# Another order for converting w_out, and six transfers on another queue, in a DeltaNet and FFN kernel

## The chip, the cores and the metric

The kernel runs on one core of a Trainium2 chip, as one launch. The metric is device time in microseconds. Three executions of the kernel before took 726.48, 727.93 and 732.02 us; their median is 727.93.

## The reference

The first half is a DeltaNet attention: for each of 4 x 8 heads a 48 x 48 state is carried over 768 time steps. The second half is a feed-forward net on the result, with a quick GELU between its two matrices.

```python
k_n = k / (norm(k) + 1e-6)
for t in range(768):
    y[t]  = q[t] @ state
    v_old = state.T @ k_n[t]
    state = state + beta[t] * outer(k_n[t], v[t] - v_old)
x = y as (3072 tokens, 384)
h = x @ w_in                    # 384 x 2048
out = (h * sigmoid(1.702 * h)) @ w_out   # 2048 x 384
```

The weights `w_in` and `w_out` arrive in 64-bit floating point. The engines compute in 32 bits, so the kernel converts each weight itself, from the two 32-bit words of its 64.

## The kernel before, in words

**The attention.** Time is cut into 6 chunks of 128 steps. A chunk and a batch make a *unit*, 24 in all, with 8 heads each (from the second chunk on, a unit takes half a chunk of two batches). Within a unit the recurrence is a triangular system per head: Gram products of the keys (`gram`, tile `G`) give the matrix, whose 32 x 32 diagonal blocks are sent through memory (`Nd`) into the tile `NT`, one block per partition, and inverted there on VectorE (`invert`: tiles `NT`, `P`, `YB`, some 60 steps). The inverses come back through memory (`Yd`) as `XB`. Then the blocks are solved one after the other: TensorE multiplies by `XB` into `psU`, ScalarE copies the result into `VU`, TensorE subtracts its part from the later blocks (`psV`, in the first chunk), ScalarE copies that into `VU`, and so on. One such round is called a hop here. The first four units are solved in two pairs, units 0 and 1 in one loop of eight hops (`path`), 2 and 3 in the next (`later`); each loop closes with `put_out`, which multiplies with the queries (`psY`) and adds into the state `ST`. Before a unit's keys are used they are divided by their norms: VectorE sums squares (`ssq`), GpSimd takes the root (`rn`), VectorE inverts it, and ScalarE or VectorE scales the keys `KN`.

**The FFN.** `hidden` multiplies 256 tokens (`xT`) by `w_in` into tiles `ph`, two rows of 128 features at a time, and ScalarE applies the GELU into `gT`. `both_written` and `written` multiply `gT` with `w_out` into `po`. In the later slots (`seven`) half of these products are done by a seven-product scheme that needs differences of blocks of `w_out`; GpSimd forms them (`combined`, line 986, into `TW`). FFN work fills TensorE wherever the attention makes it wait.

**The weights.** `w_out` is 16 blocks of 128 rows. A block of raw words takes twice the space of the converted block. Raw words therefore lie in one of two sorts of places: inside `w_out` itself, in the part of it that is converted later (`inside`: blocks 3, 4, 5, 6, 7, 12, 13), or in tiles that other data has left (`outside`: 0, 8, 11 in a tile of the tag `xT`; 1, 9, 14 and 2, 10, 15 in two tiles of the tag `M`, which unit 0 to 2 use too). `order` lists the blocks as they are converted; 4 with 5 and 6 with 7 are one piece of twice the size. A conversion is six steps: a mask (VectorE), a Relu that shifts the exponent (ScalarE), and four more on VectorE. `conversions` interleaves two pieces: the first mask of the next piece comes ahead of the last two steps of the present one, and its Relu with it. When a piece is done, `fetches` issues the transfer of the block that takes its place.

**What sets the order.** Each engine works through its own queue in program order. Most instructions are recorded in the order of the Python code (`tc.keep_in_program_order`, the helper on line 123). The conversions and the second inversion form one background generator (`background`): all pieces up to the eighth block, then `invert(1)`, then the other pieces. `fill(us)` draws so many estimated microseconds from it, so the numbers in the `fill` calls decide behind which hop a conversion step stands, on VectorE and on ScalarE alike. Operations that are not pinned (line 986, 107, 115) may be placed earlier. Transfers are issued by SyncE (`sync`), by GpSimd (`other_queue`) or by ScalarE (`beside`); a transfer that must wait for its place to be free holds up those behind it in the same queue. The functions that the change touches:

Of the kernel before, what the change touches and what calls it, by code (L numbers as in the profile page):

```python
# [18 lines left out]
def kernel(  # L19
# [21 lines left out]
    B, H, S, D = q.shape  # L41
# [9 lines left out]
    NB = C // BS  # L51
# [5 lines left out]
    HF, HM = FC // 2, DM // 2  # L57
# [24 lines left out]
    QP = [cpool.tile([128, H, DP], F32, name=f"QP{i}") for i in range(2)]  # L82
# [7 lines left out]
    def place(dst, n):  # L90

        return dst[n if n < B else n % 2] if dst is QP else dst[n % len(dst)]
# [3 lines left out]
    def segments(n):  # L96

        c, m = units[n]
        if n < B:
            return [(slice(0, C), m, slice(c * C, (c + 1) * C))]  # L100
        at = c * C + m // 2 * CH
        return [(slice(u * CH, (u + 1) * CH), m % 2 * 2 + u, slice(at, at + CH)) for u in range(2)]

    def load(n, pairs, dma=nc.sync.dma_start):
        for dst, src in pairs:
            for rows, b, t in segments(n):
                dma(  # L107
                    out=place(dst, n)[rows, :, 0:D],
                    in_=src[b, :, t, :].rearrange("h p d -> p h d"),
                )  # L110
# [10 lines left out]
    def pinned(op):  # L121

        return lambda *a, **kw: tc.keep_in_program_order(op(*a, **kw))  # L123
# [12 lines left out]
    sync, beside = pinned(nc.sync.dma_start), pinned(nc.scalar.dma_start)  # L136
# [17 lines left out]
    def warm(n, after=None):  # L154
        ps = ps_moe.tile([128, 256], F32, tag="moe", name="ps_warm")
        if after is not None:
            after(ps[:, 0:1], 0.0)
        for _ in range(n):
            pe.matmul(ps, lhsT=ones[:, 0:128], rhs=ones, start=True, stop=True)
# [11 lines left out]
    def as_raw(words, shape):  # L171
        a, b = shape
        return words.rearrange("p (j n o) -> p j n o", j=a, n=b)

    def as_rows(raw):
        return raw.bitcast(moe_w_in.dtype).rearrange("p j n o -> p j (n o)")
# [35 lines left out]
    places, slots = {}, {}  # L212
    inside = {3: 6, 4: 8, 5: 10, 6: 12, 7: 14, 12: 14, 13: 10}
    outside = {0: "xT", 8: "xT", 11: "xT", 1: "M", 9: "M", 14: "M", 2: "M2", 10: "M2", 15: "M2"}
    order = [0, 1, 2, 3, 4, 5, 6, 7, 8, 13, 9, 10, 12, 11, 14, 15]

    def fetch_out(f):

        if f in outside:
            slot = outside[f]  # L220
            if slot not in slots:
                slots[slot] = wk.tile([128, 2 * DM], I32, tag=slot[:2].strip("2"), name="raw", bufs=4 if slot[0] == "M" else 3)
            words = slots[slot]
        else:
            words = raws[:, inside[f] * DM : (inside[f] + 2) * DM]
        places[f] = as_raw(words, (1, DM))
        sync(out=as_rows(places[f])[:, 0], in_=moe_w_out[f * 128 : (f + 1) * 128, :])

    def conversion(dst, raw, shape):

# [47 lines left out]
    done = set()  # L278

    def conversions():  # L280

        whole = list(pieces())

        def begin(i):
            dst, raw, shape, name = whole[i]
            ops = conversion(dst, places[name[1]] if raw is None else raw, shape)
            return ops, next(ops)

        after, cost = begin(0)
        next(after)  # L290
        yield cost
        for i in range(len(whole)):
            ops = after
            yield next(ops)
            yield next(ops)
            if i + 1 < len(whole):
                after, cost = begin(i + 1)
                yield cost
                next(after)
            yield next(ops)  # L300
            cost = next(ops)
            done.add(whole[i][3])
            fetches.pop(whole[i][3], lambda: None)()
            yield cost

    fetches = {
        ("in", 1): lambda: fetch_in(3, js=(2,)),
        ("in", 3): lambda: [fetch_out(f) for f in (4, 5, 6, 7)],
        ("in", 4 * KC - 1): lambda: fetch_out(3),
        ("out", 4): lambda: fetch_out(13),  # L310
        ("out", 6): lambda: fetch_out(12),
    }
# [3 lines left out]
    def background():  # L316

        converting = conversions()
        while ("out", order[HF - 2]) not in done:
            yield next(converting)  # L320
        yield from invert(1)
        done.add("inverse")
        yield from converting

    behind = background()

    def fill(us):
        while us > 0:
            us -= next(behind, us)
# [126 lines left out]
    def gram(n):  # L456

        return gram_whole(n) if n < B else gram_halves(n)
# [44 lines left out]
    def turn(n):  # L503
        kTs[n] = wk.tile([128, NP, 128], F32, tag="kT", name="kT", bufs=5)
        transposed(home(n), kTs[n])

    def load_diagonal(n, Nd, dma):

        b = units[n][1]
        dma(  # L510
            out=NT[b * NB * H : (b + 1) * NB * H].rearrange("d i k -> d (i k)"),
            in_=Nd.rearrange("(d r) -> d r", r=BS * BS),
        )
# [15 lines left out]
    def send_blocks(n, others=(), dma=sync):  # L529

        G = ready[n][2]
        Nd = dram.tile([H * C * BS], F32, tag="Nd", name="Nd", bufs=4)
        to = Nd.rearrange("(h p k) -> p h k", p=C, k=BS)
        for blk in range(NB):
            u = slice(blk * BS, (blk + 1) * BS)
            k = u if n < B else slice(blk % 2 * BS, (blk % 2 + 1) * BS)
            (beside if blk in others else dma)(out=to[u], in_=G[u, :, k])  # L537
        return Nd
# [543 lines left out]
    def written(c, b0, gT):  # L1082

        for i in range(HB):
            b = b0 + i
            po = ps_moe.tile([128, DM], F32, tag="moe", name="po")
            for f in range(FC):
                pe.matmul(
                    po, lhsT=gT[f // FQ][:, f % FQ, i * C : (i + 1) * C], rhs=w_out[:, f, :],
                    start=(f == 0), stop=(f == FC - 1),  # L1090
                )
                if f % 2 == 1 and f < FC - 1:
                    yield 1.3
            o = wk.tile([128, DM], F32, tag="o", name="o")
            act.copy(o, po)
            nc.sync.dma_start(out=out[b * S + c * C : b * S + (c + 1) * C, :], in_=o)
            yield 1.3
# [54 lines left out]
    def together(solves, belows):  # L1152

        solves = [(X, blk) for X, blk in solves if X]
        belows = [(X, blk) for X, blk in belows if X]
        psU = bank("psU") if solves else None
        psRs = [bank("psR") if X.n >= B else None for X, blk in belows]
        for h in range(H):
            for X, blk in solves:
                X.solve(blk, h, psU)  # L1160
            for (X, blk), psR in zip(belows, psRs):
                X.below(blk, h, psR)
        for X, blk in solves:
            X.solved(blk, psU)
        for (X, blk), psR in zip(belows, psRs):
            X.rest(blk, psR)
# [79 lines left out]
    other_queue = pinned(nc.gpsimd.dma_start)  # L1246
    betas = beta.rearrange("b h (c k j) -> (b h) c k j", k=NB, j=BS)
    for blk in range(NB):
# [3 lines left out]
        out=YB, in_=YB, compare_op=ALU.not_equal, fill=1.0, base=0,  # L1252
# [38 lines left out]
    for at in range(B):  # L1291
        for u in range(2):
            for half_ in range(2):
                lane = at * BS + u * 2 + half_
                other_queue(
                    out=bL[lane : (at + 1) * BS : NB],
                    in_=betas[(at % 2 * 2 + u) * H : (at % 2 * 2 + u + 1) * H, 1:, at // 2 * 2 + half_, :],
# [30 lines left out]
    def put_out(s):  # L1328
        s.queries()
        s.outputs(True, lambda: fill(1.7))  # L1330
        steps.pop(s.n)
# [4 lines left out]
    for i in range(2 * NB):  # L1336
        together(*next(path))
        if i in (1, 3):
            turn(B + HB + i // 2)
        if i in (4, 5):  # L1340
            gram(B + HB + i - 4)
            Ndx.append(send_blocks(B + HB + i - 4))
        if i < 2 * NB - 1:
            warm(NU if i == 2 else NU // 2 if i in (1, 3, 4, 5) else 2 * NU // 3)
        fill(2.1)
    put_out(pair[0])
    for X in pair[2:]:
        X.gather()
    load_diagonals(Ndx)
# [2 lines left out]
    fill(1.9)  # L1352
    put_out(pair[1])
    load(8, ((KN, k),), sync)
    for f in range(1, 3):
        fetch_out(f)
    for n in range(B, B + 2):
        load(n, ((QP, q),), sync)

    ffn = []  # L1360

    def feed(n=1):
        for _ in range(n):
            while ffn and next(ffn[0], None) is None:
                ffn.pop(0)
# [3 lines left out]
    for i in range(1, 2 * NB):  # L1369
        together(*next(later))  # L1370
        if i < 4:
            warm(NU if i < 3 else NU // 2)
        if i > 2:
            feed()
        fill(2.7)
    for s in pair[2:]:
        put_out(s)
        feed()
# [42 lines left out]
        fill(0.1)  # L1421
    for n in (2 * B, 2 * B + 1):
        load_diagonal(n, Nds[n], sync)
    fill(4)
    queue = [both, written(*units[HB], gTs[1])]
    early_banks.close()
    late["one"] = ctx.enter_context(
# [40 lines left out]
```

## Time and profile before

| | before |
|---|---|
| median of 3 executions | 727.93 us |
| the profiled execution | 727.72 us |
| its span | 726.0 us |
| mean granted TensorE clock | 0.971 |
| TensorE, matmuls | 679.5 us busy, 94% of the span |
| VectorE | 457.3 us, 63% |
| GpSimd | 255.9 us, 35% |
| ScalarE | 236.8 us, 33% |

How to read the rows of the profile: a row of a timeline is start, length (both in us), engine, line, operation, tiles as out<-in, partitions and elements, and how many instructions were merged (x). A bracket at its end gives the idle time of the engine just ahead of it and what ended that. A row of the chain of waits is start, length, and what the chain passes through. A row of the stage table is the stretch, its length, then for TensorE matmuls, TensorE weight loads, VectorE, ScalarE and GpSimd the busy us with their instructions in brackets, then the granted TensorE clock as a share of full speed, the busy share of the DMA engines, and GB/s. A matmul in 32 bits appears as two records, so a row of six is three matmuls. PE is TensorE, DVE VectorE, ACT ScalarE, POOL GpSimd, SP SyncE; SPq rows are the issuing of transfers.

### The profile page before, as it was taken

Reading aid. Unit: us, or ns where it says so; the run is one execution under the profiler, and the core shown is the slowest. Engines: PE = TensorE matmul, PEld = TensorE weight load, DVE = VectorE, ACT = ScalarE, POOL = GpSimd, SP = SyncE. Lnnn points to the kernel's source line nnn. Section 1 sums busy time; section 2 is a strip of 40 time slices with the busy share of each in tenths; the row PEclk is TensorE's granted clock in tenths of the full one; section 3 lists DMA queues with packets and bytes.
Section 4 is the critical chain, followed back from the end, with each engine's and each line's share of the span. In section 5 each row is a group of like instructions: output and inputs, shape, how many; then the busy total and the mean of one; then the engine's idle time right before and its main releaser. Section 6 shows DMA issues by size and latency. Waiting matters only on the chain.

```text
span 726.0 us, 20454 instructions
## 1 busy us (share of the span) xinstructions
PE 679.5 (94%) x8787; PEld 583.7 (80%) x8787; DVE 457.3 (63%) x869; ACT 236.8 (33%) x565; POOL 255.9 (35%) x267
## 2 busy tenths in 40 slices
PE   9188969989899999999999999999999999999997
PEld 7156758765567898898988888988988988989997
DVE  4799839984476499398498497696694892110000
ACT  3363635371233413413313323333233223222120
POOL 6085002030146652642652642732621402304032
PEclk9677989999999999999999999999999999999999
DMA  9897553342122312314213224123123111000100
GB/s 170 144 184 157 161 147 81 76 97 71 34 63 48 73 34 62 65 30 85 42 36 82 39 36 93 27 44 74 38 44 60 34 26 31 7 23 2 28 0 23
DMA packets 129179, 46.66 MB, mean 64 GB/s; under 512 B 118848, under 2 KB 123584, under 8 KB 129088
## 3 DMA queue, kind: packets, MB, share of 16 engines
q1 hardware_dynamic: 125280, 39.89, 26.9%
q0 software_dynamic: 2624, 5.07, 3.2%
q8 instruction: 69, 1.13, 0.7%
q10 hardware_dynamic: 1184, 0.39, 0.2%
q14 instruction: 22, 0.18, 0.1%
HBM read 33.13 MB, written 11.01 MB: 61 GB/s over the span
## 4 chain that ended last, share of the span: by engine, by line
PE 50%; DVE 30%; DMA 7%; issue 4%; ACT 4%; SPq 2%; POOL 2%; DVEq 0%; ACTq 0%; POOLq 0%
PE ph L123 21%; PE po L123 16%; DVE P L123 12%; DVE YB L123 6%; PE four L123 4%; DVE NT L123 3%; DMA NT<-Nd 3%; PE psU L123 3%; PE ps_warm L123 3%; DVE VU L123 2%; DVE w_out L123 2%; PE psT L123 2%; DMA Nd<-G 2%; PE psR L123 1%; SPq L537 1%
## 5 line engine op out<-in xcount | busy, mean ns | idle before, releaser
L123 PE MATMUL ph<-xT,w_in 128*128 128x256 f32 x1152 | 259.8, 383 | 1.8 <-ACT gT L123 1.5
L123 PEld LDWEIGHTS ph<-xT,w_in 128*128 128x128 f32 x1152 | 216.3, 191 | 33.0 <-ACT gT L123 1.9
L123 PE MATMUL po<-w_out,gT 128*128 128x192 f32 (+1 forms) x720 | 139.2, 348 | 8.7 <-DVE o L123 5.0
L986 POOL TENSOR_TENSOR gT<-gT 128x512 f32<-128x512 f32 x80 | 105.7, 1330 | 102.2 <-ACT gT L123 68.1
L123 PEld LDWEIGHTS po<-w_out,gT 128*128 128x128 f32 x720 | 118.5, 191 | 21.9 <-issue 7.4
L123 DVE TENSOR_TENSOR P<-NT,YB 64x2 f32<-64x2 f32 (+9 forms) x200 | 123.7, 619 | 5.8
L123 ACT ACTIVATE gT<-ph 128x512 f32<-128x512 f32 x90 | 53.6, 597 | 144.3 <-PE ph L123 143.0
L123 DVE TENSOR_REDUCE YB<-P 64x2 f32<-64x2 f32 (+9 forms) x200 | 81.8, 409 | 6.9
L123 PE MATMUL po<-TW,gT 128*128 128x192 f32 x480 | 82.3, 328 | 0.5 <-ACT o L123 0.5
L123 PEld LDWEIGHTS po<-TW,gT 128*128 128x128 f32 x480 | 78.0, 190 | 1.8 <-ACT o L123 1.1
L123 ACT COPY VU<-psU 32x384 f32<-32x384 f32 x96 | 45.1, 470 | 54.1 <-PE psU L123 48.2
L852 POOL TENSOR_SCALAR_AFFINE_SELECT M<-M 64x512 f32<-64x512 f32 x40 | 29.7, 742 | 89.6 <-ACT M L123 88.3
L123 DVE TENSOR_TENSOR o<-o,po 128x192 f32<-128x192 f32 x40 | 13.8, 346 | 73.8 <-PE po L123 44.5
L123 DVE TENSOR_TENSOR VU<-VU,psR 32x384 f32<-32x384 f32 x40 | 22.1, 554 | 41.3 <-PE psR L123 40.6
L123 PEld LDWEIGHTS psU<-VU,XB 32*32 32x32 f32 x1536 | 28.5, 106 | 20.5 <-ACT VU L123 10.1
L123 DVE TENSOR_TENSOR NT<-NT,bL 64x1024 f32<-64x1024 f32 (+1 forms) x9 | 12.0, 1328 | 47.3 <-DMA NT<-Nd 47.3
L107 POOL DMA_DIRECT2D KN<-in_k_dram x24 | 17.0, 711 | 69.6 <-PE four L123 69.6
L123 PE MATMUL psU<-VU,XB 32*32 32x48 f32 x1536 | 33.7, 204 | 7.9 <-ACT VU L123 7.9
L123 DVE TENSOR_TENSOR VU<-VU,four 128x384 f32<-128x384 f32 x19 | 10.5, 552 | 45.2 <-issue 33.2
L346 POOL TENSOR_TENSOR rn<-ssq,half 128x8 f32<-128x8 f32 x12 | 22.1, 1846 | 47.1 <-DVE ssq L123 47.1
L123 ACT COPY xT<-four 128x256 f32<-128x256 f32 (+1 forms) x40 | 13.1, 328 | 75.9 <-DVE ST L123 73.5
L123 ACT COPY M<-four 128x512 f32<-128x512 f32 x19 | 11.1, 586 | 78.5 <-DVE VU L123 69.7
(133 smaller groups left out, 788.6 us busy)
## 6 DMA issues: line engine op xcount, KB each, us to landing
QP<-in_q_dram SPq DMA_DIRECT2D x40, 96.0 KB, 2.8
VU<-in_v_dram SPq DMA_DIRECT2D x40, 96.0 KB, 3.7
out_dram<-o SPq DMA_DIRECT2D x40, 96.0 KB, 2.2
raw<-in_moe_w_out_dram SPq DMA_DIRECT2D x9, 384.0 KB, 3.7
NT<-Nd SPq DMA_DIRECT2D x24, 128.0 KB, 2.4
XB<-Yd SPq DMA_DIRECT2D x24, 128.0 KB, 2.6
Yd<-NT SPq DMA_DIRECT2D x22, 128.0 KB, 2.1
Nd<-G SPq DMA_DIRECT2D x86, 32.0 KB, 1.7
```

The source lines that it names most:

```text
L107: dma(out=place(dst, n)[rows, :, 0:D], in_=src[b, :, t, :].rearrange("h p d -> p h d"),)
L123: return lambda *a, **kw: tc.keep_in_program_order(op(*a, **kw))
L346: nc.gpsimd.tensor_tensor(rn, ssq, half, op=ALU.pow)
L537: (beside if blk in others else dma)(out=to[u], in_=G[u, :, k])
L852: nc.gpsimd.affine_select(out=M, in_=M, compare_op=ALU.is_gt, fill=0.0, base=0, pattern=[[0, H], [1, CH]], channel_multiplier=-1,)
L986: (engine or nc.gpsimd).tensor_tensor(o, a, b, op=op)
```

## The change

The order of conversion becomes 0, 4 and 5, 3, 1, 6 and 7, 2, and then as before: the pieces 4 and 5, and 3, whose raw words lie inside `w_out`, move ahead of 1 and 2. The background loop waits for the eighth entry of the order and not the seventh, since a single block now stands last among the first eight. Blocks 1 and 2 and the queries of units 4 and 5, which SyncE fetched behind the first pair of units, are now fetched by GpSimd's queue, earlier in the code: the queries and block 1 behind the seventh hop of the first pair, block 2 behind unit 0's `put_out`. Two fill amounts change: 2.7 to 2.3 in the second pair's loop (seven times), and 4 to 8 ahead of the slots.

```diff
-    order = [0, 1, 2, 3, 4, 5, 6, 7, 8, 13, 9, 10, 12, 11, 14, 15]
-
-    def fetch_out(f):
+    order = [0, 4, 5, 3, 1, 6, 7, 2, 8, 13, 9, 10, 12, 11, 14, 15]
+
+    def fetch_out(f, dma=sync):
...
-        sync(out=as_rows(places[f])[:, 0], in_=moe_w_out[f * 128 : (f + 1) * 128, :])
+        dma(out=as_rows(places[f])[:, 0], in_=moe_w_out[f * 128 : (f + 1) * 128, :])
...
-        while ("out", order[HF - 2]) not in done:
+        while ("out", order[HF - 1]) not in done:
...
+        if i == 2 * NB - 2:
+            for n in range(B, B + 2):
+                load(n, ((QP, q),), other_queue)
+            fetch_out(1, other_queue)
         fill(2.1)
     put_out(pair[0])
+    fetch_out(2, other_queue)
     for X in pair[2:]:
         X.gather()
...
     load(8, ((KN, k),), sync)
-    for f in range(1, 3):
-        fetch_out(f)
-    for n in range(B, B + 2):
-        load(n, ((QP, q),), sync)
...
         if i > 2:
             feed()
-        fill(2.7)
+        fill(2.3)
...
-    fill(4)
+    fill(8)
     queue = [both, written(*units[HB], gTs[1])]
```

## The prediction

> **What bounds the kernel now.** I start with the stage table (busy time per engine, granted clock, DMA share), because a share over the whole span mixes stages with different limits.
>
> ```profile
> 94.00:103.00 9.00, 2.75 (x52) 2.12 (x45) 2.32 (x6) 1.56 (x3) 0.00 (x0) 0.86 0.85 178
> 103.00:113.00 10.00, 10.00 (x146) 7.76 (x140) 5.73 (x13) 5.58 (x11) 0.99 (x1) 0.79 0.42 142
> 160.00:190.00 30.00, 25.59 (x166) 14.54 (x165) 16.89 (x37) 8.03 (x18) 1.54 (x2) 0.99 0.21 53
> 190.00:400.00 210.00, 207.09 (x3040) 176.91 (x3042) 149.91 (x276) 66.69 (x161) 94.90 (x91) 0.99 0.28 57
> 400.00:640.00 240.00, 237.40 (x3403) 214.47 (x3396) 158.03 (x291) 71.71 (x172) 88.79 (x81) 1.00 0.21 42
> 640.00:726.00 86.00, 81.93 (x576) 75.56 (x575) 4.48 (x12) 15.32 (x35) 20.10 (x16) 0.99 0.06 14
> ```
>
> The first number behind each length is TensorE's. From 190 us on it is busy 526.4 of 536 us, so what starts earlier at 190 ends earlier at 726, microsecond for microsecond. Before that there is a hole: at 94 to 103 us TensorE works 2.75 of 9 us, VectorE 2.32, ScalarE 1.56, GpSimd nothing, while the DMA engines are 0.85 busy. Everybody waits for a transfer. The timelines of VectorE, ScalarE, TensorE and SyncE and the chain of waits (the row with "DMA raw") say which one.
>
> ```profile
> 92.93 0.36 DVE L123 TENSOR_SCALAR raw<-raw 128x384 int32<-128x384 int32 x1
> 100.61 0.36 DVE L123 TENSOR_SCALAR w_out<-raw 128x384 int32<-128x384 int32 x1 [7.31 <-DMA raw<-in_moe_w_out_dram]
> 101.00 0.62 ACT L123 ACTIVATE w_out<-w_out,low 128x384 int32<-128x384 int32 x1 [7.96 <-DVE w_out L123]
> 101.64 0.47 ACT L123 COPY VU<-psU 32x384 f32<-32x384 f32 x1
> 94.95 1.46 PE L123 MATMUL ph<-xT,w_in 128*128 128x256 f32 x6
> 102.66 0.28 PE L123 MATMUL psU<-VU,XB 32*32 32x48 f32 x1 [6.25 <-ACT VU L123]
> ```
>
> ```profile
> 89.53 4.63 SPq L123 DMA_DIRECT2D xT<-last  x6
> 94.26 1.35 SPq L123 DMA_DIRECT2D KN<-in_k_dram  x2
> 95.66 1.09 SPq L123 DMA_DIRECT2D raw<-in_moe_w_out_dram  x2
> 96.80 3.33 SPq L123 DMA_DIRECT2D QP<-in_q_dram  x4
> 100.22 1.28 SPq L123 DMA_DIRECT2D w_out<-in_moe_w_out_dram  x1
> ```
>
> ```profile
> 95.66 4.93 DMA raw<-in_moe_w_out_dram
> ```
>
> Block 1 of w_out, second to be converted, is only issued at 95.66, behind eight other transfers in SyncE's queue, and lands 4.93 us later. VectorE waits for it, ScalarE's Relu of the same block waits for VectorE, and behind that Relu in ScalarE's queue stands the copy of U without which the next solve hop of units 2 and 3 can't start: TensorE idles 6.25 us. That hole is the first place to look for a gain.
>
> **The change part by part.** TensorE's order is the same in both programs; what moves is the order on VectorE and ScalarE, and six transfers.
>
> *Blocks 4 and 5 second.* VectorE takes them up at 93.3, where block 0's third step, the row at 92.93, ends. Their words were fetched long before:
>
> ```profile
> 73.14 1.79 SPq L123 DMA_DIRECT2D w_out<-in_moe_w_out_dram  x4
> DMA to landing us min/median/max: 3.1/6.1/8.4
> 107.95 1.49 PE ph L123 x6
> 110.24 1.51 PE ph L123 x6
> 111.66 0.86 PE L123 MATMUL psU<-VU,XB 32*32 32x48 f32 x16
> 104.09 2.93 PE L123 MATMUL ph<-xT,w_in 128*128 128x256 f32 x6
> ```
>
> Issued by 74.93, landed by 83.3 even at the slowest 8.4, wanted at 93.3. Their Relu now stands behind the two copies that the next hop needs, so that hop starts when TensorE has done its half tile of the FFN: 94.95 + 1.46 = 96.41 in place of 102.66, **6.25 us** earlier. Then the clock: hop plus half tile take 110.24 - 107.95 = 2.29 us once it is back, but the three from 102.66 to 111.66 took 9.00 us, as the half tile at 104.09 took 2.93 and not 1.49. Without the hole they take 6.87, so the last hop starts at 103.3, **8.4 us** earlier. (The Trainium skill, "TensorE: Matmul & The Clock Gate", Part 1, says that about 3.4 us without activity halve the clock. The 0.86 and 0.79 above agree, and by it any new wait shorter than that costs only its own length.)
>
> *Block 3 third.* The raws and queries leave SyncE's queue, so block 3's fetch moves from 100.22 into block 1's old place, 95.66, and with that row's 4.93 us lands at 100.6. One VectorE step and its Relu (0.36 and 0.62, the rows at 100.61 and 101.00) end at 101.6. That Relu stands ahead of the copy behind the hop of 96.41 + 2 x 2.29 = 101.0, which ends at 101.8. So it costs nothing, with 0.2 us of cover: at the slowest landing, 8.4, the copy is 3.3 us late; at 3.1 nothing is gained, since TensorE sets the pace. I take 0.
>
> *VectorE up to the inversion.* The same eight blocks stand ahead of it, with the same busy time.
>
> ```profile
> 108.19 0.56 DVE L123 SCALAR_TENSOR_TENSOR w_out<-raw,w_out 128x384 int32<-128x384 int32 x1 [3.96 <-ACT w_out L123]
> 113.22 1.60 DVE L123 SCALAR_TENSOR_TENSOR w_out<-w_out 128x768 int32<-128x768 int32 x1 [0.29 <-ACT w_out L123]
> 122.56 1.22 DVE L123 TENSOR_TENSOR NT<-NT,bL 128x1024 f32<-128x1024 f32 x1
> 127.05 0.54 DVE L123 TENSOR_REDUCE ssq<-ksq 128x8 f32<-128x384 f32 x1
> 151.72 1.22 DVE L123 TENSOR_TENSOR NT<-YB,bL 128x1024 f32<-128x1024 f32 x1
> ```
>
> 7.31 + 3.96 + 0.29 = 11.6 us of waiting go. In their place I find, step by step along the new order: 1.3 for the Relu of 4 and 5 (behind the two copies, done at 96.3), 2.4 for block 3 (98.2 to 100.6), 1.2 for the two sums into the state, which wait for ScalarE's copies behind each unit's last solve, 0.4 for block 2's Relu behind a Gelu: 5.3. One sum of key squares (0.5) now stands ahead too. The inversion starts 11.6 - 5.3 - 0.5 = 5.8 us earlier, at 116.8. It lasts 152.94 - 122.56 = 30.4, plus one more small step on a norm, some 0.35: it ends at 147.6 and not 152.9.
>
> *Norms ahead of conversions.* Seven fills of 2.3 for 2.7 let VectorE's background work run 2.8 us less far ahead, so the steps of the key norms come earlier among it. Before, the last norm, at 157.87, stood 4.9 us behind the inversion, after block 8's and half of block 13's conversion; now it follows it directly, at 147.9.
>
> ```profile
> 157.87 0.17 DVE L123 TENSOR_SCALAR rn<-rn 128x8 f32<-128x8 f32 x1
> 133.07 1.56 PE L123 MATMUL ph<-xT,w_in 128*128 128x256 f32 x6 [1.47 <-ACT gT L123]
> 157.90 0.69 PE L123 MATMUL psG<-kT 48*64 48x64 f32 x32 [1.29 <-ACT kT L123]
> 159.92 0.81 PE L123 MATMUL po<-w_out,gT 128*128 128x384 f32 x2
> 161.85 9.94 PE L123 MATMUL po<-w_out,gT 128*128 128x384 f32 x30 [1.12 <-ACT TW L123]
> 171.72 0.87 PE L123 MATMUL psU<-VU,XB 32*32 32x48 f32 x32
> ```
>
> From that norm to the big run of output products is 161.85 - 157.87 = 4.0 us (scale the keys, evict Gram blocks, a Relu, the last Gelu). So the products could start at 147.9 + 4.0 = 151.9. TensorE must be there too: it was ready at 160.73; less 8.4, less the 1.47 at 133.07 (ScalarE's scaling waited for a norm that now comes after three inversion steps and not ten), it is ready at 150.9. The later one holds; with 0.2 for the wait for kT, which stays about as it was, the products start at **152.1, 9.7 us earlier**. The new slots' first solves follow 9.9 us behind, at 162; the inversion's result, needed there, lands some 7 us behind its end as before, at 155.
>
> ```profile
> PE po L123 <- DVE w_out L123: 2.6, 2, 1.9
> ```
>
> *Fill 8 for 4 ahead of the slots* makes up for the fills dropped earlier: in both programs three Relus (of 13, 9, 10) stand between the inversion and the first copy of the slots. What they hold up is that copy; they are done at 156, the copy is due at 163: 6 us of cover. So the ping-pong of products and conversions behind it, where TensorE waits 2.6 of the 4.4 us that it idles from 160 to 190, comes back unchanged: 0; were it gone, 2.6 would be gained.
>
> *GpSimd's queue.* It gets four query loads and two raws.
>
> ```profile
> 104.31 0.99 POOL L986 TENSOR_TENSOR TW<-w_out 128x384 f32<-128x384 f32 x1 [38.96 <-DVE w_out L123]
> 54.05 4.08 DMA TW<-in_moe_w_in_dram
> 66.00:68.00 2.00, 1.72 (x56) 1.32 (x43) 1.97 (x4) 0.49 (x1) 0.00 (x0) 1.00 0.50 74
> 68.00:70.00 2.00, 0.65 (x48) 0.65 (x52) 1.97 (x3) 1.87 (x4) 0.00 (x0) 0.93 0.18 24
> ```
>
> GpSimd idles 38.96 us up to 104.31, so queries and block 1 go out as it falls idle, at 65.4, into DMA engines that are 0.50 and 0.18 busy, and land by about 75 (its own queue's 4.08 us, doubled). Block 2's place is unit 0's M, read until 85: it lands by 93 and is wanted at 111.5. Queued behind it on GpSimd are only differences of w_out, due after 103. I take 0; the bounds are up to 1 us lost if the extra transfers delay the hops of 69 to 80, and 0.5 gained if SyncE's shorter queue helps.
>
> A page speaks against this part: the Trainium skill, "DMA: Bandwidth & Descriptors", section "Issuing engines are not separate DMA queues", holds that issuing from several engines saves only the sequencer's issue time. SyncE's rows of 95.66 and 96.80 show that time, 1.09 + 3.33 = 4.4 us, which is block 3's advance; by the page the move alone is worth that much there and no faster transfers, and the sum above claims no more of it.
>
> **Sum.** -9.7 us. The profiled execution took 727.72 us (726.0 of span, 1.7 around it; both in the table above), 0.2 under the median of 727.93; it becomes **718.0**.
>
> **The rivals.**
> - *Block 3 is the new late block.* For it: only 0.2 us of cover, and key loads just ahead of it in the queue. Against: four query loads fewer beside it. At the slowest landing 3.3 us of the gain go: 721.3.
> - *The gain of the products shrinks to VectorE's own* 5.8 us, since norms and ScalarE's order cost again what they did (waits 1.47, 1.29, 1.12 come back): 721.9.
> - *The second piece does not run ahead*, because 4 and 5 wait for something I don't see, or the hole opens again one block later: about 727.
> - *Slower:* GpSimd builds its descriptors slowly while VectorE is busy (1.97 of 2 us in the rows at 66 and 68), and block 2 is late. The place is its Relu, ahead of a Gelu on ScalarE. From 111.5 on each microsecond late is lost, 9.7 us late, from 121.2 on, the kernel is slower than before; 18 us late it takes 718 + 18 = 736. Against it: transfers of that queue at 54.05 landed in 4.08 us with VectorE just as busy, and cover is 18 us to begin with. (The Trainium skill, the same page, section "SWDGE vs HWDGE vs iDMA", says that VectorE's two-port modes lock GpSimd out of the memory that holds its descriptors; no run shown here measures that.)
>
> **How the numbers follow.** Forecast 0.62 (own range 715 to 720.6), late block 3 0.18, VectorE's gain only 0.10, no change 0.03, slower 0.07. One per cent, about what a measurement of this kernel can tell from no change, is 7.3 us: faster means under 720.65. That is the forecast's case and a third of block 3's: 0.68; within 1%: 0.25; slower: 0.07. The range runs from 714.5 (the 2.6 of the ping-pong and the 0.5 of SyncE's queue gained too, rounded out) to 723.5 (block 3 late and part of VectorE's loss).
>
> **What would show it.** Right: no VectorE row waiting over 3 us for a raw between 93 and 122; the hop of 102.66 at about 96.4; clock 1.00 at 103 to 113; the inversion starting near 117; the products at about 152, first slot solves at 162; TensorE full from 181 on. Wrong: ScalarE's block 3 Relu ending after 102; a GpSimd transfer landing after 100; norms at the end of the inversion waiting for GpSimd; idle TensorE behind 181.

## The result, and the profile after

The changed kernel took 723.82 us (median of 20 executions, 716.52 to 728.15) beside 729.35 us for the kernel before (20 executions, 724.83 to 737.43). The ratio is 0.9896, with a 95% interval from 0.9863 to 0.9929: 1.0% faster, or 7.6 us. It is the ratio of the means, 721.86 and 729.43 us, without the executions over 1.5% above the fastest of their kernel (one and two), so it is not the quotient of the medians. The profiled execution took 716.79 us, 10.9 less than the profiled execution of before. The two gains differ because the executions of one and the same program spread over two groups some 7 us apart; the experiments come back to that, and the sizes below are made independent of it.

The stage table of the changed kernel, with the same columns as before's:

```profile
94.00:103.00 9.00, 9.00 (x153) 7.03 (x152) 6.55 (x11) 5.84 (x12) 1.25 (x1) 1.00 0.49 149
103.00:113.00 10.00, 10.00 (x97) 8.53 (x96) 7.90 (x13) 4.81 (x12) 2.00 (x2) 1.00 0.19 38
160.00:190.00 30.00, 26.93 (x349) 15.96 (x346) 15.80 (x40) 9.50 (x21) 2.86 (x4) 0.94 0.24 64
190.00:400.00 210.00, 206.56 (x3018) 179.42 (x3018) 150.24 (x271) 68.07 (x162) 100.62 (x96) 1.00 0.27 54
```

The hole is gone: TensorE works 9.00 of 9 us at 94 to 103, where it worked 2.75, and the clock is 1.00 where it was 0.86 and 0.79. From 190 us on TensorE is as full as before (206.56 of 210 us, for 207.09).

The timelines of the changed kernel (start, length, engine, line, operation; in brackets the idle time ahead of the row and what ended it):

```profile
64.43 2.94 POOL L123 DMA_DIRECT2D QP<-in_q_dram  x4
67.36 0.60 POOL L123 DMA_DIRECT2D raw<-in_moe_w_out_dram  x1
83.79 0.56 POOL L123 DMA_DIRECT2D raw<-in_moe_w_out_dram  x1 [15.83 <-issue]
87.30 0.25 ACT L123 COPY last<-psY 128x128 f32<-128x128 f32 x1
93.64 1.29 SPq L123 DMA_DIRECT2D w_out<-in_moe_w_out_dram  x1
97.88 0.36 DVE L123 TENSOR_SCALAR w_out<-w_out 128x384 int32<-128x384 int32 x1 [1.60 <-DMA w_out<-in_moe_w_out_dram]
101.56 0.86 PE L123 MATMUL psU<-VU,XB 32*32 32x48 f32 x16
115.30 1.22 DVE L123 TENSOR_TENSOR NT<-NT,bL 128x1024 f32<-128x1024 f32 x1
144.86 1.22 DVE L123 TENSOR_TENSOR NT<-YB,bL 128x1024 f32<-128x1024 f32 x1
146.00 0.16 DVE L123 TENSOR_SCALAR rn<-rn 128x8 f32<-128x8 f32 x1
149.98 9.94 PE L123 MATMUL po<-w_out,gT 128*128 128x384 f32 x30 [1.58 <-ACT TW L123]
159.86 0.87 PE L123 MATMUL psU<-VU,XB 32*32 32x48 f32 x32
238.13 0.88 PE L123 MATMUL psU<-VU,XB 32*32 32x48 f32 x64
```

And two rows of the timelines of before, which the prediction did not need:

```profile
88.96 0.25 ACT L123 COPY last<-psY 128x128 f32<-128x128 f32 x1
249.91 0.88 PE L123 MATMUL psU<-VU,XB 32*32 32x48 f32 x64
```

The copy `last<-psY` at 87.30 and 88.96 closes the first pair of units; I call its start **T0**. Ahead of it only the transfers on GpSimd's queue are new, yet T0 differs by 1.66 us between the two profiles. In the seven profiles of the changed kernel and its variants below in which the clock stays at 1.00 from 63 us to T0, T0 lies between 87.17 and 89.08, so the 1.66 can't be put down to the change. Steps are therefore compared from T0 on:

| from T0, us | before | changed | gain | forecast |
|---|---|---|---|---|
| last hop of units 2 and 3 | 22.70 | 14.26 | 8.4 | 8.4 |
| start of the inversion | 33.60 | 28.00 | 5.6 | 5.8 |
| run of output products | 72.89 | 62.68 | 10.2 | 9.7 |
| first solves of the slots | 82.76 | 72.56 | 10.2 | 9.9 |
| solves of a later slot (249.91, 238.13) | 160.95 | 150.83 | 10.1 | |
| end of the span | 637.0 | 627.8 | 9.2 | 9.7 |

### The profile page after: what moved, and what is told of

It is laid out like the page before. It is cut to its first block, busy times and chain, and to the rows that moved or that the text cites. A ratio compares the mean times of both kernels' runs of the same rounds, so it can differ in the third digit from the quotient of the medians.

```text
span 715.1 us, 20458 instructions
## 1 busy us (share of the span) xinstructions
PE 675.9 (95%) x8787; PEld 581.5 (81%) x8787; DVE 457.3 (64%) x869; ACT 236.8 (33%) x565; POOL 259.6 (36%) x273
## 3 DMA queue, kind: packets, MB, share of 16 engines
q0 software_dynamic: 2976, 6.25, 3.8%
## 4 chain that ended last, share of the span: by engine, by line
PE 53%; DVE 29%; DMA 6%; ACT 4%; issue 4%; SPq 3%; POOL 0%; DVEq 0%; ACTq 0%; POOLq 0%
PE ph L123 22%; PE po L123 16%; DVE P L123 12%; DVE YB L123 6%; PE four L123 4%; DVE NT L123 3%; PE psU L123 3%; PE ps_warm L123 3%; DVE VU L123 2%; DMA NT<-Nd 2%; PE psT L123 2%; DMA Nd<-G 2%; SPq L123 2%; PE psR L123 1%; DVE w_out L123 1%
## 5 line engine op out<-in xcount | busy, mean ns | idle before, releaser
L107 POOL DMA_DIRECT2D KN<-in_k_dram x24 | 17.1, 713 | 70.1 <-PE four L123 69.0
L123 DVE TENSOR_TENSOR VU<-VU,four 128x384 f32<-128x384 f32 x19 | 10.5, 552 | 45.5 <-issue 32.9
L123 ACT COPY M<-four 128x512 f32<-128x512 f32 x19 | 11.1, 585 | 78.1 <-DVE VU L123 69.3
L123 DVE TENSOR_TENSOR P<-NT 64x512 f32<-64x512 f32 (+7 forms) x50 | 34.1, 682 | 1.6
```

The costliest lines, as they stand in the source:

```text
L107: dma(out=place(dst, n)[rows, :, 0:D], in_=src[b, :, t, :].rearrange("h p d -> p h d"),)
```

## The experiments

**The theory** after the result was the prediction's: the transfers and the order close the hole, and the smaller fills, which bring the norms forward, give the rest. **The first rival**: the six transfers carry everything, and order and fills nothing.

Of each profile four distances from T0 are given: to the start of the inversion, to the run of output products, to the solves at 249.91 of before, and to the end.

| kernel | inversion | products | solves | end | time against before, 95% |
|---|---|---|---|---|---|
| before | 33.6 | 72.9 | 161.0 | 637.0 | |
| changed | 28.0 | 62.7 | 150.8 | 627.8 | 0.9896 [0.9863, 0.9929] |
| `again` (unedited) | 29.4 | 64.1 | 151.7 | 628.0 | 0.9864 [0.9803, 0.9926] |
| `after_2` (unedited) | 28.3 | 63.0 | 150.5 | 626.9 | 0.9892 [0.9843, 0.9940] |
| `order_only` | 33.1 | 72.4 | 160.5 | 635.8 | 1.0006 [0.9964, 1.0048] |
| `queue_only` | 25.3 | 64.6 | 151.2 | 628.2 | 0.9899 [0.9830, 0.9968] |
| `old_fills` | 25.4 | 64.7 | 151.3 | 627.7 | 0.9952 [0.9910, 0.9993] |
| `warm` | 28.0 | 62.7 | 150.2 | 626.6 | 0.9831 [0.9735, 0.9927] |
| `warm_2` | 28.0 | 62.7 | 150.2 | 627.7 | 0.9840 [0.9791, 0.9890] |
| `cold` | 28.8 | 63.5 | 151.0 | 627.4 | 0.9916 [0.9873, 0.9959] |
| `warm_before` | 33.0 | 72.2 | 160.4 | 637.1 | 0.9938 [0.9902, 0.9973] |
| `warm_queries` | 29.3 | 64.0 | 152.2 | 630.0 | 0.9830 [0.9753, 0.9906] |
| `warm_blocks` | 31.4 | 66.1 | 153.6 | 630.9 | 0.9815 [0.9741, 0.9890] |
| `warm_block3` | 29.6 | 64.3 | 151.8 | 628.9 | 0.9876 [0.9827, 0.9926] |

The changed kernel alone lies between 626.9 and 628.0 at the end, so less than about 1 us is not told apart there; at the products it lies between 62.7 and 64.1. Each row is one profile. The times against before carry the two groups of executions with them and are wider.

### The order alone

```diff
-    order = [0, 1, 2, 3, 4, 5, 6, 7, 8, 13, 9, 10, 12, 11, 14, 15]
+    order = [0, 4, 5, 3, 1, 6, 7, 2, 8, 13, 9, 10, 12, 11, 14, 15]
...
-        while ("out", order[HF - 2]) not in done:
+        while ("out", order[HF - 1]) not in done:
```

The kernel before with these two edits; the transfers stay on SyncE's queue, the fills as they were.

> Only the order of the pieces is new; transfers and fill amounts are those of before. My theory: block 3, now third, is still fetched behind blocks 1, 2 and the queries at about 100.2 us and lands near 105; its Relu stands ahead of a copy of the next hop, so the hole moves from block 1 to block 3 and the time is within 2 us of before. Rival, the order alone fills the hole: 9 to 10 us faster.

Measured: no difference in time, 1.2 us less from T0 to the end. Stage table, TensorE's waits and SyncE's timeline of this kernel:

```profile
103.00:113.00 10.00, 4.81 (x76) 3.71 (x75) 3.45 (x5) 2.64 (x6) 1.22 (x1) 0.92 0.75 189
113.00:123.00 10.00, 10.00 (x65) 7.76 (x64) 8.18 (x15) 4.21 (x10) 2.01 (x3) 0.57 0.23 76
```

```profile
PE psU L123 <- ACT VU L123: 5.2, 1, 5.2
```

```profile
100.53 1.67 SPq L123 DMA_DIRECT2D raw<-in_moe_w_out_dram  x2
102.25 2.78 SPq L123 DMA_DIRECT2D QP<-in_q_dram  x4
105.13 0.57 SPq L123 DMA_DIRECT2D w_out<-in_moe_w_out_dram  x1
```

Block 3, now third in the order, is issued behind the two raws and the four queries, 11.1 us after T0, and the hole opens there: TensorE waits 5.2 us, and behind the hole the clock is 0.57. The order by itself only moves the hole by one block.

### The six transfers alone

```diff
     path, later = hops(*pair[:2]), hops(*pair[2:])
...
+        if i == 2 * NB - 2:
+            for n in range(B, B + 2):
+                load(n, ((QP, q),), other_queue)
+            fetch_out(1, other_queue)
         fill(2.1)
     put_out(pair[0])
+    fetch_out(2, other_queue)
...
-    for f in range(1, 3):
-        fetch_out(f)
-    for n in range(B, B + 2):
-        load(n, ((QP, q),), sync)
```

The kernel before with the transfers moved to GpSimd's queue, in the old order and with the old fills.

> Only the six transfers move to GpSimd's queue; order and fill amounts are those of before. My theory: blocks 1 and 2 land by 75 and 93 us, block 3 takes the freed place on SyncE, so the hole of 6.25 us closes without the new order; but the norms stand behind conversions as before (4.9 us behind the inversion), so the products begin near 156.5 us and the time is 5 us under before. Rival, the new order is needed: the hole stays, within 2 us of before. Rival, the transfers carry everything: 9 to 10 us under.

Measured: 0.9899 of before, and 8.8 us less from T0 to the end (637.0 - 628.2); the expected loss against the full change (products at 156.5, 5 us under before in all) is not there; at the products 1.9 us of it show. Stage table and VectorE's timeline:

```profile
94.00:113.00 19.00, 19.00 (x295) 15.56 (x294) 15.37 (x28) 11.08 (x24) 2.99 (x3) 1.00 0.43 130
```

```profile
114.87 1.22 DVE L123 TENSOR_TENSOR NT<-NT,bL 128x1024 f32<-128x1024 f32 x1
```

GpSimd issues block 1 at 68.05, where SyncE issued it at 95.66 in the kernel before. With it fetched that early the old order has no hole either: TensorE works 19.00 of 19 us. The inversion even starts earlier than in the changed kernel, 25.3 us after T0 for 28.0.

### The old fills

```diff
-        fill(2.3)
+        fill(2.7)
...
-    fill(8)
+    fill(4)
```

The changed kernel with the two fill amounts of before.

> The changed kernel with the old fill amounts, 2.7 and 4. My theory: the Relu of block 3 stands one hop earlier on ScalarE and holds it up by some 2 us, and the norms come behind conversions again, so the products begin 4 to 5 us later than in the changed kernel: 4 to 6 us under before. Rival, the fill amounts do nothing: as the changed kernel, within 1 us.

Measured: 627.7 from T0 to the end, as the changed kernel. The timeline shows why the norms are worth less than thought:

```profile
94.52 0.27 ACT L123 COPY last<-psY 128x128 f32<-128x128 f32 x1
119.94 1.22 DVE L123 TENSOR_TENSOR NT<-NT,bL 128x1024 f32<-128x1024 f32 x1
149.09 1.22 DVE L123 TENSOR_TENSOR NT<-YB,bL 128x1024 f32<-128x1024 f32 x1
155.25 0.16 DVE L123 TENSOR_SCALAR rn<-rn 128x8 f32<-128x8 f32 x1
159.23 9.94 PE L123 MATMUL po<-w_out,gT 128*128 128x384 f32 x30 [1.12 <-ACT TW L123]
```

With the old fills the last norm does stand 4.9 us behind the end of the inversion (155.25 for 149.09 + 1.22), as in the kernel before. But the inversion starts 2.6 us earlier (25.4 for 28.0): from T0 to it VectorE waits 3.1 us and not 5.2, and one sum of key squares (0.5) less stands ahead of it. The products lose 2.0 us against the first profile of the changed kernel (64.7 for 62.7) but only 0.6 against `again` (64.1); at the later solves and at the end no clear difference is left.

From the products to the later solves the changed kernel takes 88.1 us in its first profile and 87.5 in `again`; with the old fills it takes 86.6. The first profile has 3.4 us at half clock there (174.9 to 178.3; the 0.94 in its stage table), `again` has none, which goes with the 0.6 between them. Of the other 0.9, TensorE's waits for `w_out` are 0.6: 3.3 us in `again`, 2.7 here.

The time itself, 0.9952, lies above that of the unedited kernel, but 8 of its 10 executions belong to the upper of the two groups, which are decided ahead of T0, where this edit changes nothing. The first rival holds, within the 1 us that is not told apart: the transfers carry the gain.

### The same kernel again: two groups of times

> The changed kernel again, unedited. If its timeline is what made the gain, the products of w_out (the run of 30 that began at 161.85 us before) begin near 150 us again, TensorE waits nowhere more than 1.6 us between 94 and 150 us, and the span is about 11 us shorter than before. If part of that was a lucky start of the one execution, the start (the last copy of the first pair's result, 88.96 us before, 87.30 after) is back at 89 us and the span is 9.5 us shorter.

Measured: 715.95, 717.08, 717.47 and 719.73 us, and then 725.73 and 726.01. With the first 20 executions and the 6 of `after_2` there are 32 of the unedited kernel: 14 between 715.95 and 720.03 (mean 718.0, mean clock of the execution 0.973 to 0.981), 18 between 723.21 and 728.15 (mean 725.1, clock 0.960 to 0.969), none between. The kernel before, beside these and the later kernels, has 51: 25 under 730 (mean 727.2, clock 0.966 to 0.976) and 26 above (mean 734.2, clock 0.955 to 0.965). Its times show no such gap (729.36, 730.22 and 731.45 follow on each other), so its division at 730 is a choice. Lower against lower the change is worth 9.2 us, upper against upper 9.1, and from T0 in the profiles 9.2. The 10.9 of the two profiled executions has 1.7 of chance in it, and the 7.6 by the ratio comes from sets in which 8 of the changed kernel's 20 and 11 of before's 20 were in the lower group.

The profile of `again` caught an execution of the upper group (725.73 us). Its stage table:

```profile
72.00:76.00 4.00, 3.27 (x79) 2.50 (x82) 3.66 (x7) 2.82 (x6) 0.00 (x0) 0.75 1.00 251
76.00:84.00 8.00, 8.00 (x167) 6.22 (x160) 3.36 (x7) 3.71 (x9) 0.00 (x0) 0.50 0.63 193
84.00:94.00 10.00, 10.00 (x84) 6.80 (x79) 6.66 (x14) 3.46 (x8) 0.56 (x1) 0.50 0.41 103
```

The same stretches of the first profile of the changed kernel (716.79 us):

```profile
72.00:76.00 4.00, 3.93 (x143) 3.43 (x144) 3.63 (x8) 2.92 (x7) 0.00 (x0) 1.00 0.77 194
76.00:84.00 8.00, 7.23 (x163) 5.75 (x161) 6.38 (x13) 5.54 (x15) 0.21 (x1) 1.00 0.80 213
84.00:94.00 10.00, 10.00 (x262) 8.20 (x261) 8.99 (x19) 6.28 (x16) 0.35 (x1) 1.00 0.35 93
```

The clock is 0.50 from about 74 to 94 us, in the hops of the first pair, and T0 comes at 95.99 and not at 87.30. From T0 to the end the two are alike (628.0 and 627.8). Just ahead of the drop TensorE has two waits, here from the timeline of `again`:

```profile
69.14 0.23 PE L123 MATMUL psU<-VU,XB 32*32 32x48 f32 x1 [0.81 <-ACT VU L123]
72.73 0.23 PE L123 MATMUL psU<-VU,XB 32*32 32x48 f32 x1 [1.29 <-ACT VU L123]
```

The length of these waits alone doesn't decide. The same two, 0.93 and 1.29 us, stand in the first profile of the changed kernel, where the clock stays at 1.00; in `order_only` they are 0.30 and 1.28, and it falls.

Stage tables in stretches of half a microsecond show more. In each of the profiles, from 21 to 260 us, all changes of the clock lie on one grid with steps of 3.41 us, which is shifted from execution to execution. In `again` half clock lasts from 73.97 to 94.45, six steps; in `order_only` from 73.84 to 90.90, five; in the kernel before it begins at 69.72, 100.44 and 189.19, which are 9 and 26 steps apart. And a drop does not by itself make the upper group. In the profile of `queue_only`, which took 719.46 us, it ends after one step:

```profile
72.00:74.00 2.00, 1.25 (x51) 1.19 (x52) 1.97 (x4) 0.99 (x3) 0.00 (x0) 0.92 1.01 304
74.00:76.00 2.00, 2.00 (x18) 1.26 (x19) 1.70 (x4) 1.85 (x4) 0.00 (x0) 0.50 0.95 230
76.00:78.00 2.00, 2.00 (x82) 1.84 (x77) 1.97 (x4) 0.65 (x2) 0.00 (x0) 0.73 0.98 350
```

The lost 0.08, 0.50 and 0.27 of 2 us each, at half clock, make 3.4 us. The profile of the kernel before also has one step there. The four profiles of the upper group (`again`, `order_only`, `old_fills`, `cold`) have five to seven, and the other eight none. What ends the low clock after one step or only after five stays open.

### Filling or opening these two waits

```diff
-            warm(NU if i == 2 else NU // 2 if i in (1, 3, 4, 5) else 2 * NU // 3)
+            warm(23 if i == 2 else 14 if i == 1 else NU // 2 if i in (3, 4, 5) else 2 * NU // 3)
```

`warm` issues matmuls whose result nobody reads; with this line there are 14 and 23 of them behind the second and third hop, for 6 and 12. It was put into the changed kernel (twice, on two chips) and into the kernel before.

> The changed kernel with more idle-filling matmuls behind the second and third hop of the first pair (14 for 6 and 23 for 12; each takes about 0.11 us beside waits of 0.9 and 1.3 us for ScalarE's VU). Theory (the two sets of times of one kernel come from the clock, which these two waits tip to half from 74 us on in some executions): the granted clock stays at 0.97 or more from 72 to 94, T0 (start of the first pair's COPY last<-psY) is at 86.5 to 88.5, the time 715 to 718 in nearly every execution, with a spread under 4 us; from T0 to the end of the span 627.5 to 628.5. Rival (the two times come from elsewhere and the clock only follows): the times still spread from 716 to 726, T0 anywhere from 87 to 96.

> The kernel before with the same additional matmuls. Theory: 724 to 727 in nearly every execution, T0 at 86.5 to 88.5, span less T0 636 to 637.5; so the change is worth 9 us (ratio 0.987 to 0.988) once the clock is the same on both sides. Rival: spread from 724 to 736 as before.

Measured: in the three profiles of these kernels the clock stays at 1.00 from 63 us to T0, here from the stage table of `warm`:

```profile
72.00:76.00 4.00, 4.00 (x82) 3.29 (x83) 3.90 (x7) 2.29 (x6) 0.00 (x0) 1.00 1.04 277
76.00:84.00 8.00, 7.36 (x216) 5.86 (x215) 5.47 (x11) 6.68 (x15) 0.00 (x0) 1.00 0.70 202
```

The executions of `warm` were 717.37, 717.64 and 718.82, and one of 726.82 at a clock of 0.965. T0 was 89.08, and 89.30 in `warm_before`, both later than expected. The kernel before gains by it (0.9938): 9 of the 10 executions of `warm_before` lie under 730 us, of the 13 beside them on the same chip 4. Its median of 727.97 is above the 724 to 727 expected.

The unedited and the filled kernel side by side on one chip, and the opposite edit:

```diff
-            warm(NU if i == 2 else NU // 2 if i in (1, 3, 4, 5) else 2 * NU // 3)
+            warm(3 if i == 2 else 1 if i == 1 else NU // 2 if i in (3, 4, 5) else 2 * NU // 3)
```

> The changed kernel unedited, beside its warmed forms on one chip. Theory of the clock: executions near 717 to 719 (clock 0.978 or more) and near 723 to 726 (0.964 to 0.970), both present; median above that of the warmed kernel by 2 to 5.

> The changed kernel with 14 and 23 idle-filling matmuls for 6 and 12, a second time. Theory: at least 7 in 10 executions at 716 to 720 with clock 0.975 or more, median 718, ratio to before 0.983 to 0.988. Rival (the additional matmuls only shifted chance): as many executions above 722 as in the unedited kernel.

> The changed kernel with 1 and 3 idle-filling matmuls behind the second and third hop of the first pair, for 6 and 12. Theory of the clock: TensorE idles 1.4 and 2.3 us there, the granted clock goes to 0.50 in every execution from about 72 on, T0 95 to 97, time 724 to 727 with clock 0.963 to 0.970 and none under 721. Rival (chance, not these idle stretches): some executions at 717 to 719 as before.

Measured: medians of 724.0 for `after_2` and 721.4 for `warm_2`. `after_2` has 2 of 6 in the lower group, `warm_2` 3 of 6 under 720, and two near the foot of the upper group (723.25 and 723.88), at clocks of 0.974 and 0.971. With the four of `warm`, 6 of 10 lie under 720, against 13 of 32 unedited: fewer than the 7 in 10 expected, and no proof. `cold` had 7 of 8 between 725.02 and 726.38 and one at 718.80. Its timeline and stage table:

```profile
69.03 0.23 PE L123 MATMUL psU<-VU,XB 32*32 32x48 f32 x1 [2.23 <-ACT VU L123]
72.60 0.28 PE L123 MATMUL psU<-VU,XB 32*32 32x48 f32 x1 [1.59 <-ACT VU L123]
```

```profile
68.00:72.00 4.00, 1.99 (x67) 1.33 (x67) 3.90 (x7) 2.56 (x6) 0.52 (x1) 0.67 1.02 238
```

With these waits at 2.23 and 1.59 us the clock falls from the first of them on. `warm_before` shows that the two waits bear on the clock. For `cold` the numbers are weaker: 7 of 8 in the upper group, where 18 of 32 unedited are, could come by chance in about one case of ten. And the waits don't decide alone: one execution of `cold` was as short as the lower group, at a mean clock of 0.975, and four of the ten of `warm` and `warm_2` were above 720. What decides in those wasn't seen, as no profile fell on one of them.

### Half of the transfers each

Both kernels hold the additional matmuls, and so are read beside `warm` and `warm_2` (626.6 and 627.7 from T0 to the end). In `warm_queries` only the four query transfers go through GpSimd's queue:

```diff
         if i == 2 * NB - 2:
             for n in range(B, B + 2):
                 load(n, ((QP, q),), other_queue)
-            fetch_out(1, other_queue)
...
-    fetch_out(2, other_queue)
...
     load(8, ((KN, k),), sync)
+    for f in range(1, 3):
+        fetch_out(f)
```

In `warm_blocks` only the two blocks do:

```diff
         if i == 2 * NB - 2:
-            for n in range(B, B + 2):
-                load(n, ((QP, q),), other_queue)
             fetch_out(1, other_queue)
...
     load(8, ((KN, k),), sync)
+    for n in range(B, B + 2):
+        load(n, ((QP, q),), sync)
```

> The changed kernel with the additional matmuls, but only the four transfers of queries on GpSimd's queue; blocks 1 and 2 are fetched by SP behind the first outputs, as before, so two issues (1.1 to 1.7 us) stand ahead of block 3's on SP. Theory (the gain is that SP reaches block 3 early: 6.3 us after T0 in the changed kernel, 11.1 with all six ahead of it): issued 8.0 after T0, landed 12.4, 1.8 later than in the changed kernel, of which 0 to 1 is covered: span less T0 628.5 to 630, time 717 to 719. Rival (blocks 1 and 2 themselves must come early): hole at block 1 or 2 instead, span less T0 632 or more.

> The changed kernel with the additional matmuls, but only blocks 1 and 2 on GpSimd's queue; the four transfers of queries on SP behind the first outputs, as before, so 2.8 to 3.3 us of issues stand ahead of block 3's on SP. Theory: block 3 issued 9.2 after T0, landed 13.5, 2.9 late, 2 to 3 of it on the path: span less T0 629.5 to 631, time 718 to 720. Rival (the queries' place is of no matter): span less T0 as in the changed kernel, 627.5 to 628.5.

Timelines of `warm_queries`, then of `warm_blocks`:

```profile
87.92 0.24 ACT L123 COPY last<-psY 128x128 f32<-128x128 f32 x1
95.94 0.38 SPq L123 DMA_DIRECT2D w_out<-in_moe_w_out_dram  x1
100.79 0.36 DVE L123 TENSOR_SCALAR w_out<-w_out 128x384 int32<-128x384 int32 x1 [3.87 <-DMA w_out<-in_moe_w_out_dram]
```

```profile
87.17 0.25 ACT L123 COPY last<-psY 128x128 f32<-128x128 f32 x1
97.68 0.57 SPq L123 DMA_DIRECT2D w_out<-in_moe_w_out_dram  x1
102.14 0.36 DVE L123 TENSOR_SCALAR w_out<-w_out 128x384 int32<-128x384 int32 x1 [5.99 <-DMA w_out<-in_moe_w_out_dram]
104.08 0.86 PE L123 MATMUL psU<-VU,XB 32*32 32x48 f32 x16 [1.08 <-ACT VU L123]
```

In the changed kernel VectorE takes block 3 up 10.6 us after T0 (97.88 - 87.30); with two raws ahead of it on SyncE's queue 12.9, with four queries ahead of it 15.0. The end is 630.0 and 630.9 after T0, so between 2 and 4 us of the gain go, by one profile each; the ratios of `warm`, `warm_queries` and `warm_blocks`, from four executions each, don't tell the three apart (0.9831, 0.9830 and 0.9815). Both halves of the move are needed in the new order, because both stand ahead of block 3. No hole opens at blocks 1 and 2, though in `warm_queries` they came from SyncE's queue as late as before. The first came out at the upper edge of what was expected; in the second block 3 was issued 10.5 us after T0 and not 9.2, and still ended within the expected 629.5 to 631, so what a microsecond of delay costs is not settled by these two.

### Block 3 through GpSimd's queue as well

```diff
-        ("in", 4 * KC - 1): lambda: fetch_out(3),
+        ("in", 4 * KC - 1): lambda: fetch_out(3, other_queue),
```

The warmed kernel, in the hope of the 1.6 us that VectorE still waits for block 3.

> The warmed kernel, with block 3 fetched by GpSimd's queue too. It no longer stands behind SP's KN and xT: issued about 91 to 92 (4 after T0) for 95.4 in the warmed kernel (6.3 after T0), landed 9 to 10 after T0 for 10.6; VectorE's wait of 1.58 falls to 0 to 0.6. Theory (what the transfers bought is VectorE's idle time before the inversion): 1.0 to 1.6 us less from T0 to the end, 625 to 625.8; time 716.5 to 717. Rival (TensorE sets the pace there now): no change, 626.6.

Measured: 628.9 from T0 to the end, 1.2 to 2.3 more than the warmed kernel. Timeline of this kernel:

```profile
91.11 0.69 POOL L123 DMA_DIRECT2D w_out<-in_moe_w_out_dram  x1 [6.70 <-DVE w_in L123]
95.72 0.67 PE L123 MATMUL ph<-xT,w_in 128*128 128x256 f32 x2 [1.34 <-DMA xT<-last]
98.55 1.00 POOL L986 TENSOR_TENSOR TW<-w_out 128x384 f32<-128x384 f32 x1 [6.75 <-DVE w_out L123]
```

VectorE's wait for block 3 is gone, and the first difference of `w_out` on GpSimd starts 1.6 us earlier after T0 (11.2 for 12.8 in `warm_2`). But the 384 KB, issued at 91.11, now run beside the small `xT<-last` transfers that SyncE issues from 87.93 to 92.0. The slowest of these takes 4.2 us to land, for 3.1 in `warm_2`, and TensorE waits 1.34 us for them, which it did not do in the warmed kernel. Neither theory had that: a wait that cost nothing was exchanged for one that TensorE pays.

No version here is shown to be faster than the changed kernel. The lowest ratios, 0.9815 to 0.9840, are those of `warm_blocks`, `warm_queries`, `warm` and `warm_2`. The first three come from a chip on which the unedited kernel was not run, and the interval of `warm_2` overlaps with that of `after_2` (0.9892) on the same chip.

## Why the prediction was right, point by point

The forecast of 718.0 us, 9.7 less than before, was right in size: 9.2 from T0, and the gains of the hop, the inversion and the products each within 0.5 us of their forecast. How it is made up was right only in part, and that the sum came out is in part luck.

- **Blocks 4 and 5 second.** Right: the last hop of units 2 and 3 is 8.4 us earlier, 6.25 of it the hole and the rest the clock, which stays at 1.00. But `queue_only` closes the hole in the old order too. The step described what happens and not what is needed for it.
- **The clock in it.** The Trainium skill, "TensorE: Matmul & The Clock Gate", Part 1, was cited for a clock that halves after about 3.4 us without activity, from which I drew that a shorter wait costs only its own length. Behind the hole of 5.2 us in `order_only` the trace agrees (0.57). In `again` it differs: the longest wait ahead of the drop is 1.29 us, and the measurement decides.
- **Block 3 third.** Right: issued 6.3 us after T0, and TensorE does not wait for it; VectorE does, 1.6 us for the forecast 2.4. The rival of a late block 3 was a real risk and not an idle one: the raws (1.1 to 1.7 us of issues) or the queries (2.7 to 3.3) ahead of it, in the two half moves, cost 2 to 4 us.
- **VectorE up to the inversion.** Right for this kernel, 5.6 us for 5.8, and its waits add up to 5.2 for the forecast 5.3. It is not what the gain would be without the fills: with the old ones it is 8.2, since the smaller fills themselves put the start off by 2.6 us.
- **Norms ahead of conversions.** This is the step that failed. I put 3.9 us of the 9.7 on the fills, as if VectorE's 5.8 stood without them. The runs show 0.6 to 2.0 us at the products and nothing clear at the end. Without the fills the products gain 8.2 and not 5.8, and the transfers alone give 8.8 at the end. The term was too large by about what the one ahead of it was too small, so the sum fitted.
- **From 190 us on, microsecond for microsecond.** Not quite. The 10.2 us of the products are 9.2 at the end, and with the old fills the 8.2 of the products are 9.3 (637.0 - 627.7). From the products to the later solves alone the profiles take 86.6 to 88.1 us, by TensorE's waits and by whether a step at half clock falls there.
- **Fill 8 for 4.** I put it at 0. TensorE's waits for `w_out` in the ping-pong were 2.6 us before; its list of waits has 2.4 in the first profile of the changed kernel and 3.3 in `again`, which has no half clock there:

```profile
PE po L123 <- DVE w_out L123: 2.4, 4, 1.1
PE po L123 <- DVE w_out L123: 3.3, 4, 1.1
```

This fill was never changed without the other, so which of the two lengthens the waits stays open.
- **GpSimd's queue.** Costed at nothing, and no cost is seen: five issues from 64.43 on, block 2 at 83.79, and the next row of GpSimd waits for VectorE and not for a transfer. The rival of a late block 2, slower than before, did not come. The other rule cited, that several issuing engines save only the issue time (the Trainium skill, "DMA: Bandwidth & Descriptors", section "Issuing engines are not separate DMA queues"), explains block 3's 4.8 us (6.3 after T0 for 11.1 in `order_only`, where the issues ahead of it take 1.67 + 2.78 us). It leaves out that in `queue_only` block 1 no longer waits for its turn in a queue whose earlier transfers wait for the first outputs, and that was the hole.
- **The sum against the measured median.** The forecast was made against one profiled execution, and that was in the lower group of before; 718.0 is the mean of the changed kernel's lower group. By the ratio, 0.9896 of the 727.93 the forecast started from, the kernel takes 720.4, within the range of 714.5 to 723.5. Its plain median of 723.82 lies 0.3 us above the range, in the upper group, which the prediction knew nothing of. That 718.0 is met so exactly by the lower group's mean is chance.

## What to carry to other kernels

A late transfer is first a question of what stands ahead of it in its queue. Moving the early, independent transfers to a queue whose engine is idle gave 8.8 us here, where the whole change gave 9.2, while reordering the consumers moved the hole from one block to the next. When two edits together are costed as a sum, run each with the other taken away, because a term that comes before may already hold part of the one behind. And before a profiled execution is compared with another, look whether they agree ahead of the first edit; if not, measure from a row there.

## What the runs showed of the hardware

- One program has two groups of times, 7 us apart (718.0 and 725.1; 727.2 and 734.2). In the four profiles of the upper group TensorE's granted clock is 0.50 for 17 to 24 us, somewhere between 69 and 95; in the ten of the lower it is 1.00 there or 0.50 for 3.4 us. In `again` waits of 0.81 and 1.29 us go ahead of the drop, and in the step of 3.41 us just ahead of it TensorE is busy 2.12; in the first profile of the changed kernel a step with the same 2.12 (69.10 to 72.51) brought no drop.
- In every profile the clock changes only on a grid of 3.41 us: the half-clock stretches between 21 and 260 us are 3.4, 6.8, 10.2, 17.1, 20.5 or 23.9 us long. The grid is shifted from execution to execution, so the same waits fall differently into its steps; whether this makes the two groups is not shown.
- The low clock holds although TensorE is busy 8.00 of 8 and 10.00 of 10 us in `again`. By the Trainium skill, "TensorE: Matmul & The Clock Gate", Part 1, about 3.4 us of steady work end it. The single steps in before and `queue_only` agree with that; the 20.5 us in `again` do not. What ends it, and what chooses the group where the waits are filled, stays open.
- In `warm_block3` a transfer of 384 KB is issued 2.5 us earlier after T0 (3.8 for 6.3 in `warm_2`), beside transfers of 16 KB; the slowest of these lands 1.1 us later after its issue, and TensorE waits 1.34 us. One profile shows it.
